# An attention and long-convolution kernel on Trainium2: the inverse transform's leftover matmuls as a step of their own, and a new order of all steps

## The chip, the cores and the metric

The kernel runs on one core of one Trainium2 chip. A core has a matrix engine (TensorE, in profiles PE, with its weight loads shown as PEld), three engines for elementwise work (VectorE or DVE, ScalarE or ACT, GpSimd or POOL), and SyncE (SP), which here only issues transfers. The matrix engine writes to PSUM, a memory of eight banks; DVE and ACT read results out of it. Each engine executes its own instructions in order and waits on semaphores for the others. The metric is the time of one execution in device microseconds, median of several runs.

## The reference, cut to what matters

Batch 8, 8 heads, 576 positions, head size 64. The first half is attention with a feature map of exponentials, the second a gated convolution by Fourier transforms along the 576 positions.

```
def phi(x):
    proj = np.einsum('bhsd,df->bhsf', x, w_phi)
    proj = proj - np.max(np.abs(proj), axis=-1, keepdims=True)
    return np.concatenate([np.exp(proj), np.exp(-proj)], axis=-1)
q_p, k_p = (phi(q), phi(k))
kv = np.einsum('bhsf,bhsd->bhfd', k_p, v)
z = np.sum(k_p, axis=2)
num = np.einsum('bhsf,bhfd->bhsd', q_p, kv)
den = np.einsum('bhsf,bhf->bhs', q_p, z)[..., None] + 1e-06
x = (num / den) as (8, 576, 512)
...
proj = x @ w_proj
x1, x2, x3 = (proj[..., :D].copy(), proj[..., D:2 * D].copy(), proj[..., 2 * D:].copy())
X2 = np.fft.rfft(x2, n=S, axis=1)
H = np.fft.rfft(filter_fft, n=S, axis=0)[None, :, :]
x2_conv = np.fft.irfft(X2 * H, n=S, axis=1)
y = x1 * x2_conv * x3
return (y @ w_out).astype(np.float32)
```

## The kernel before, in words

All of the work is a list of 1,538 words, the table `PLAN`. A word such as `I,3,1@2` names a method of the class `Kernel`, its arguments (first the batch, 0 to 7, then a chunk) and, after `@`, the PSUM bank that it uses. The method `run` walks through the list once and calls them, and each call issues its instructions to one engine. Nothing else orders the work: an engine executes its words as they stand in the list, and the framework adds the semaphores that the data and the banks need. So the list is the schedule of five engines at once, batches are interleaved in it, and the words also say which engine does a copy out of PSUM (`KVe,ACT,0,1`, `KVe,DVE,0,1`).

The methods that matter here, by batch:

- Attention. `load` and `loadh` bring q, k and v from memory (issued by POOL); `trh` transposes them by DMA (SP), in batch 0 `pt` does it on PE. `Pk`, `Qn`, `Pkt` and `Qnt` project k and q for the maxima `maxk` and `maxq` (DVE), `Pq` and `Pqt` project q again in the other layout, `ex`, `exkt` and `exqt` are the exponentials (ACT), `vs` scales v (POOL), `KV` forms the key-value sums, `KVe` copies them out, `NE` and `NEt` apply them to q, `rc` and `xn` divide (DVE).
- Forward. `f1` and `f2` add and subtract rows (POOL, some on DVE), `Fs` and `Ft` transform into the same two PSUM banks, `Fe` copies the spectrum XF out, `Xl` gathers its last columns. `X2` projects the spectrum, `Y1` multiplies by the filter, `m3` adds two products into T0 and T2; T4 is the product of the last 128 frequencies, 64 for each parity.
- Inverse and output. `I` transforms T0, T2 and T4 back for 128 channels: for each parity e one bank, two matmuls on T0 or T2 and one on T4. `Ie` copies one bank out (ACT), `Ip` and `Im` add and subtract (DVE), `X1`, `X3` with their tails `X1t`, `X3t` are the two gates, `tm` and `ym` multiply, `O` applies w_out, `Oe` copies out and `st` stores (SP).
- `wz` are matmuls on zeros that fill PE's time at the start; `Ff`, `H` and `He` prepare the filter in the first 50 us.

Two kinds of matmuls alternate on PE. `Pk`, `Qn`, `Pq`, `KV` and `Ft` contract over 64 rows and come in pairs, one on rows 0 to 63 and one on rows 64 to 127; the others contract over 128 rows. In `I` the T4 part multiplies all 128 rows of T4 for each parity by a table whose other 64 rows are zero: `inv` 4 and 5 get their sines with a scale column that is zero on the other half (lines 473 to 475). The class also has `It` and `Is`, the same work as two methods with T4's part first over 64 rows; no word of the list before calls them.

## Time and profile before

| | |
|---|---|
| median of 3 runs | 293.64 us |
| lowest, highest | 292.83 us, 295.11 us |
| span of the profiled execution | 291.2 us |
| instructions in the span | 10275 |
| granted clock of TensorE, mean | 0.996 |

The runs are timed from outside, so they stand above the span, which reaches from the first to the last instruction of one execution. The page's second part cuts that span into 40 slices of 7.3 us; each digit is the busy share of a slice in tenths.

```profile
PE   6688999998999999999999999999999899999992
DVE  6997898999889998998888987888999988787771
ACT  4999999987958778996897978967668988641421
POOL 8388794999968899999997999867949759955130
```

PE is full from the sixth slice nearly to the end, but in the first five it is not, and there ACT shows nines. The digits of DVE fall only at the very end. A busy share says nothing of who waits for whom; for that one reads, stage by stage, which engine has no idle time left. The chain that ended last, by engine and line:

```profile
PE 71%; DVE 3%; ACT 2%; issue 1%; DVEq 0%; ACTq 0%
PE ps L917 17%; PE ps L895 11%; PE ps L1016 10%; PE ps L970 8%; PE ps L773 5%; PE ps L787 4%; PE ps L876 3%; PE ps L926 2%; PE ps L670 2%; PE ps L636 2%; PE ps L643 2%; PE ps L676 2%; PE ps L869 2%; DVE mq L716 1%; PE ps L796 1%
```

L970 is the matmul of `I`, 8% of the chain; L869 is `Ft`, L917 the projections `X1` and `X3`, L895 `X2`, L1016 `O`.

### The profile page before, as it was taken

To read this page: it belongs to the slowest core of one execution; us is meant where nothing else is said; L and a number is where in the kernel's file an instruction comes from. 1 tells how busy PE (TensorE), PEld (TensorE's weight loads), DVE (VectorE), ACT (ScalarE), POOL (GpSimd) and SP (SyncE) were. 2 spreads that over 40 slices of the span, in tenths; PEclk is the share of its full clock that TensorE was granted. 3 is DMA by queue.
4 is the path that set the end of the run, shared out by engine and by line. 5 is a ranking of instruction groups with operands and counts; after the bars stand their busy time and mean duration, and the time that the engine had idled before them with its cause. 6 is when DMAs were issued, how large, how long until landed. Compare 5 with 4: busy or idle time off the path is not lost.

```text
span 291.2 us, 10275 instructions
## 1 busy us (share of the span) xinstructions
PE 274.0 (94%) x4336; PEld 194.8 (67%) x4336; DVE 252.3 (87%) x438; ACT 221.9 (76%) x367; POOL 228.5 (78%) x187
## 2 busy tenths in 40 slices
PE   6688999998999999999999999999999899999992
...
DVE  6997898999889998998888987888999988787771
ACT  4999999987958778996897978967668988641421
POOL 8388794999968899999997999867949759955130
...
GB/s 140 230 207 175 144 204 165 139 175 181 143 192 177 163 204 159 153 119 165 122 111 156 197 169 114 163 135 191 99 14 93 84 36 2 34 108 54 69 130 184
DMA packets 72319, 40.07 MB, mean 138 GB/s; under 512 B 52496, under 2 KB 67216, under 8 KB 72272
## 3 DMA queue, kind: packets, MB, share of 16 engines
...
q10 hardware_dynamic: 320, 0.52, 0.7%
...
## 4 chain that ended last, share of the span: by engine, by line
PE 71%; DVE 3%; ACT 2%; issue 1%; DVEq 0%; ACTq 0%
PE ps L917 17%; PE ps L895 11%; PE ps L1016 10%; PE ps L970 8%; PE ps L773 5%; PE ps L787 4%; PE ps L876 3%; PE ps L926 2%; PE ps L670 2%; PE ps L636 2%; PE ps L643 2%; PE ps L676 2%; PE ps L869 2%; DVE mq L716 1%; PE ps L796 1%
## 5 line engine op out<-in xcount | busy, mean ns | idle before, releaser
L917 PE MATMUL ps<-xT,wproj 128*128 128x256 bf16 x512 | 64.0, 273 | 0.2 <-DMA wproj<-in_moe_w_proj_dram 0.2
L917 PEld LDWEIGHTS <-wproj 128*128 128x128 bf16 x512 | 48.1, 98 | 9.0 <-DMA wproj<-in_moe_w_proj_dram 0.4
L1005 POOL TENSOR_TENSOR yT<-cv,x1s 128x576 bf16<-128x576 f32 x31 | 39.4, 1279 | 15.6 <-ACT es L988 7.7
L716 DVE TENSOR_REDUCE mq<-ps 128x8 f32<-128x1024 f32 (+1 forms) x40 | 43.7, 1112 | 3.5 <-PE ps L643 1.5
L716 DVE TENSOR_REDUCE mk<-ps 128x8 f32<-128x1024 f32 (+1 forms) x40 | 44.1, 1112 | 2.9 <-PE ps L636 1.6
L758 POOL TENSOR_TENSOR vm<-vn,vm 128x1152 bf16<-128x1152 bf16 x16 | 34.3, 2152 | 7.4 <-ACT vm L752 7.4
L758 POOL TENSOR_TENSOR vp<-vn,vp 128x1152 bf16<-128x1152 bf16 x16 | 34.4, 2155 | 4.6 <-ACT vp L752 4.5
L698 ACT ACTIVATE Eqp<-ps 128x1024 bf16<-128x1024 f32 x32 | 32.9, 1038 | 6.1 <-PE ps L676 6.0
L854 POOL TENSOR_TENSOR SD<-xn 128x512 bf16<-128x512 bf16 x28 | 31.9, 1153 | 6.2 <-DVE xn L806 4.7
L1016 PE MATMUL ps<-wout,yT 128*128 128x512 bf16 x140 | 34.8, 379 | 0.1
L860 POOL TENSOR_TENSOR xf<-SD 128x512 bf16<-128x512 bf16 x26 | 29.7, 1155 | 6.4 <-DVE SD L854 5.9
L698 ACT ACTIVATE Ekp<-ps 128x1024 bf16<-128x1024 f32 x32 | 33.2, 1036 | 1.1 <-PE ps L636 0.7
L698 ACT ACTIVATE Eqm<-ps 128x1024 bf16<-128x1024 f32 x32 | 32.6, 1037 | 1.6 <-PE ps L676 0.8
L698 ACT ACTIVATE Ekm<-ps 128x1024 bf16<-128x1024 f32 x32 | 33.1, 1033 | 0.8 <-PE ps L636 0.7
L895 PE MATMUL ps<-wproj,XF 128*128 128x512 bf16 x128 | 31.6, 379 | 0.3 <-ACT x1s L298 0.3
L991 DVE TENSOR_TENSOR cv<-es,ps 128x288 f32<-128x288 f32 x64 | 26.3, 445 | 5.7 <-ACT es L988 4.4
L909 POOL TENSOR_TENSOR T<-T,T 128x1024 bf16<-128x1024 bf16 x14 | 29.6, 2127 | 1.7 <-DVE r L801 0.8
L970 PE MATMUL ps<-inv,T 128*128 128x288 bf16 x192 | 28.1, 286 | 0.7 <-DVE mq L716 0.4
L958 DVE TENSOR_TENSOR x1s<-ps,x1s 128x512 bf16<-128x512 f32 x32 | 21.8, 685 | 2.5 <-PE ps L917 1.1
L298 ACT COPY o<-ps 128x512 f32<-128x512 f32 x20 | 11.8, 600 | 14.4 <-PE ps L1016 12.0
L806 DVE TENSOR_TENSOR xn<-ps,r 128x512 bf16<-128x512 f32 x32 | 21.9, 689 | 0.9
L298 ACT CAST x1s<-ps 128x512 bf16<-128x512 f32 (+1 forms) x33 | 17.4, 540 | 6.7 <-PE ps L917 3.2
(184 smaller groups left out, 635.5 us busy)
## 6 DMA issues: line engine op xcount, KB each, us to landing
...
wproj<-in_moe_w_proj_dram POOLq DMA_DIRECT2D x3, 512.0 KB, 8.7
...
```

Source lines behind the costliest of these rows:

```text
L298: self.nc.scalar.copy(dst, src)
L698: self.nc.scalar.activation(e, p, AF.Exp, bias=0.0, scale=1.0 if g == "p" else -1.0)
L716: self.nc.vector.tensor_reduce(out=out, in_=src, axis=AX.X, op=ALU.max, apply_absolute_value=True)
L758: self.eng(eng).tensor_tensor(out=t[:, :, :, 0:64], in0=self.at("vn", b)[:, 2 * X:2 * X + 2], in1=t[:, :, :, 64:65].to_broadcast([128, 2, ...
L854: self.eng(eng).tensor_tensor(out=o[:, :, 2 * i:2 * i + 2, :], in0=x[:, :, 0:2, :], in1=x[:, :, 2:4, :], op=ALU.subtract if i else ALU.add)
L860: self.eng(eng).tensor_tensor(out=o[:, :, 2 * i:2 * i + 2, :], in0=x[:, :, 0:4:2, :], in1=x[:, :, 1:4:2, :], op=ALU.subtract if i else ALU ...
L895: self.mm(self.pb(0), l, w[:, kt, 512:1024], start=(kt == 0), stop=(kt == 3))
L909: self.eng(eng).tensor_tensor(out=Y, in0=Y, in1=self.at(f"T{2 * e + 1}", b), op=ALU.add)
L917: self.mm(o[:, d], w[:, kt, f0 + 128 * m:f0 + 128 * m + 128], y[:, 1, ::-1, ::-1] if d else y[:, 0], start=(kt == 0), stop=(kt == 3))
L970: self.mm(self.pb(e, 0, 288), l, inv[:, 2 * e + i if i < 2 else 4 + e, :], start=(i == 0), stop=(i == 2))
L1005: self.eng(eng).tensor_tensor(out=self.at("yT", b)[:, m, 0:SEQ], in0=self.turn_of("cv", (b, m)).rearrange("p x h t -> p (x h t)"), in1=sel ...
L1016: self.mm(self.pb(0), y[:, kt, 128 * c:128 * c + 128], w[:, kt, :], start=(kt == 0), stop=(kt == 3))
```

## The change

The method `I` goes. Each of its 32 words becomes two: `Is`, the four matmuls on T0 and T2, and one for T4, either `It` (24 times), which takes for each parity only that parity's 64 rows, or `Iz` (8 times), which takes all 128 rows as `I` did. Either of the two may open the PSUM sum; a set `opened` remembers which came first, and that one starts the sum. `Ft` and `Fs` get the same freedom.

```
+    def opens(self, *key):
+        new = key not in self.opened
+        self.opened.add(key)
+        return new
...
     def Fs(self, b, v):
         xf, D = self.at("xf", b), self.at("D")
+        new = self.opens("F", b, v)
         for e in range(2):
             for s in range(2):
                 self.mm(self.pb(e, 144 * s, 144 * s + 144), xf[:, v, 2 * s + e, :],
-                        D[:, 288 * e + 144 * s:288 * e + 144 * s + 144], start=False,
-                        stop=(s == 1))
+                        D[:, 288 * e + 144 * s:288 * e + 144 * s + 144], start=new and s == 0,
+                        stop=not new and s == 1)
...
-    def I(self, b, m):
-        c, inv = slice(128 * m, 128 * m + 128), self.at("inv")
-        for e in range(2):
-            Y = self.at(f"T{2 * e}", b)
-            for i in range(3):
-                l = Y[:, i, c] if i < 2 else self.at("T4", b)[:, c]
-                self.mm(self.pb(e, 0, 288), l, inv[:, 2 * e + i if i < 2 else 4 + e, :],
-                        start=(i == 0), stop=(i == 2))
-
     def It(self, b, m):
-        c, inv = slice(128 * m, 128 * m + 128), self.at("inv")
+        c, inv, new = slice(128 * m, 128 * m + 128), self.at("inv"), self.opens("I", b, m)
         for e in range(2):
             r = slice(64 * e, 64 * e + 64)
-            self.mm(self.pb(e, 0, 288), self.at("T4", b)[r, c], inv[r, 4 + e, :], start=True,
-                    stop=False)
+            self.mm(self.pb(e, 0, 288), self.at("T4", b)[r, c], inv[r, 4 + e, :], start=new,
+                    stop=not new)
+
+    def Iz(self, b, m):
+        c, inv, new = slice(128 * m, 128 * m + 128), self.at("inv"), self.opens("I", b, m)
+        for e in range(2):
+            self.mm(self.pb(e, 0, 288), self.at("T4", b)[:, c], inv[:, 4 + e, :], start=new,
+                    stop=not new)
 
     def Is(self, b, m):
-        c, inv = slice(128 * m, 128 * m + 128), self.at("inv")
+        c, inv, new = slice(128 * m, 128 * m + 128), self.at("inv"), self.opens("I", b, m)
         for e in range(2):
             for i in range(2):
                 self.mm(self.pb(e, 0, 288), self.at(f"T{2 * e}", b)[:, i, c],
-                        inv[:, 2 * e + i, :], start=False, stop=(i == 1))
+                        inv[:, 2 * e + i, :], start=new and i == 0, stop=not new and i == 1)
```

The list itself is new from its first word to its last, 1,570 words instead of 1,538. Apart from I the same steps are there, with the same arguments, but in another order, on other banks, and with some of the copies on the other engine: KVe on DVE 8 times instead of 4, Fe 10 instead of 7, Xl 3 instead of 1, yt 3 instead of 1, Ffe 1 instead of 0, and Oe 12 instead of 15. Its last line but one before, and after:

```
-Oh,7,4,0@5 Oh,7,4,1@7 st,SP,7,2,1 st,ACT,7,0,0 Oeh,DVE,7,4,0@5 sth,SP,7,4,0 Oeh,DVE,7,4,1@7
+st,ACT,7,2,0 Oe,ACT,7,0@5 Oeh,DVE,7,4,0@3 sth,SP,7,4,0 st,ACT,7,0,0 Oeh,DVE,7,4,1@4 st,SP,7,0,1
```

Three places show how instructions move. The rows give the line of the kernel's file, the operation and what is written from what; a number behind a name tells buffers apart. The first place is PE in batch 4, the end of an inverse step: before, the second half of `I` (parity 1: T2, T2, T4) with the forward step `Ft` of batch 5 behind it.

```order
L970 LDWEIGHTS T20_1165
L970 MATMUL ps_61<-inv0_69,T20_1165 128x288
L970 LDWEIGHTS T40_1167
L970 MATMUL ps_61<-inv0_69,T40_1167 128x288
L869 LDWEIGHTS xnt1_132
L869 MATMUL ps_61<-Dt0_68,xnt1_132 128x288
```

And after, at the end of the `Is` of another chunk of batch 4: its `It` follows as a step of 64 rows, and a projection of k for batch 6, also of 64 rows, stands behind it.

```order
L985 LDWEIGHTS T20_1067
L985 MATMUL ps_61<-inv0_69,T20_1067 128x288
L972 LDWEIGHTS T40_1069
L972 MATMUL ps_61<-inv0_69,T40_1069 128x288
L633 LDWEIGHTS kT0_84
L633 MATMUL ps_61<-wphi0_62,kT0_84 128x128
```

T4's matmuls have left the middle of the step and stand at its end, next to other matmuls of 64 rows. The second place is DVE in the first 60 us, where batch 0's spectrum is multiplied by the filter (T from ps and HTo or HTe) and batch 2's maxima of k are taken (mk). Before:

```order
L905 TENSOR_TENSOR T20_1165<-ps_61,HTo0_71 128x1024
L716 TENSOR_REDUCE mk0_86<-ps_61 128x2x4
L905 TENSOR_TENSOR T30_1166<-ps_61,HTo0_71 128x1024
L716 TENSOR_REDUCE mk0_86<-ps_61 128x2x4
L905 TENSOR_TENSOR T00_1163<-ps_61,HTe0_70 128x1024
L962 TENSOR_TENSOR x1s0_141<-ps_61,x1s0_141 128x4x64
L905 TENSOR_TENSOR T10_1164<-ps_61,HTe0_70 128x1024
```

After:

```order
L713 TENSOR_REDUCE mk0_86<-ps_61 128x2x4
L909 TENSOR_TENSOR T20_1067<-ps_61,HTo0_71 128x1024
L297 CAST KVs1_123<-ps_61 128x2x260
L713 TENSOR_REDUCE mk0_86<-ps_61 128x2x4
L909 TENSOR_TENSOR T00_1065<-ps_61,HTe0_70 128x1024
L909 TENSOR_TENSOR T30_1068<-ps_61,HTo0_71 128x1024
L904 TENSOR_TENSOR T40_1069<-ps_61,H50_72 128x512
```

The copy of batch 1's key-value sums, KVs1, has come from ACT into the middle of DVE's row. The third place is DVE's end, batch 7's last half sums (cv), gates (x1s), the product yT and the copies of the output o. Before:

```order
L991 TENSOR_TENSOR cv1_1171<-es1_1169,ps_61 128x9x32 x2
L300 CAST x1s0_141<-ps_61 128x2x8x32
L958 TENSOR_TENSOR x1s0_141<-ps_61,x1s0_141 128x2x8x32
L1005 TENSOR_TENSOR yT1_1173<-cv1_1171,x1s0_141 128x576
L300 COPY o1_1175<-ps_61 128x512
L300 COPY yT0_1172<-yT1_1173 128x4x64
L300 COPY o4_1178<-ps_61 128x512
L300 COPY o5_1179<-ps_61 128x256 x2
```

After:

```order
L992 TENSOR_TENSOR cv1_1073<-es1_1071,ps_61 128x9x32 x2
L962 TENSOR_TENSOR x1s0_141<-ps_61,x1s0_141 128x2x8x32
L1006 TENSOR_TENSOR yT1_1075<-cv1_1073,x1s0_141 128x576
L297 COPY o0_1076<-ps_61 128x512
L297 COPY yT0_1074<-yT1_1075 128x4x64
L297 COPY o2_1078<-ps_61 128x512
L297 COPY o3_1079<-ps_61 128x512
L297 COPY o5_1081<-ps_61 128x256 x2
```

One gate's copy has left this place for ACT, and one more copy of the output has come.

More of the change, by code (lines that the diff above doesn't have):

```diff
@@ new lines @@
+cz,DVE,1 ident sin,9 cols_a wz,32@4 wz,33@3 wz,27@0 cols_b wz,9@2 fl_load,0,1 gi_nr ang,DVE,1 wz,31@6
+fl_load,2,0 loadh,k,0,0 loadh,k,0,1 fl_load,0,0 fl_load,3,0 w_phi wz,17@3 ang,ACT,3 fl_load,1,0
+pt,q,0,0,0@4 wz,35@7 one loadh,q,0,1 pt,q,0,0,1@5 frac,3 fl_load,3,1 cols_h wz,11@3 wz,5@1 wz,0@0
+pte,ACT,q,0,0,0@4 ang,DVE,2 frac,1 pte,DVE,q,0,0,1@5 Qn,0,1@6 frac,2 ang,DVE,0 load,v,0 load,q,1
+pt,k,0,0,0@0 zeros back frac,0 sin,3 sin,2 pte,DVE,k,0,0,0@0 pt,k,0,0,1@2 sin,1 fl_loadt wz,24@3 sin,0
@@ new lines @@
+Pk,0,0@4 pte,DVE,k,0,0,1@2 wz,30@3 exz maxq,0,1@6 Qn,0,0@2 Pk,0,1@6 ex,k,p,0,0@4 maxk,0,0@4 trh,q,1,0
+pt,k,0,1,0@1 maxq,0,0@2 pt,k,0,1,1@0 load,k,1 ex,k,m,0,0@4 ex,k,m,0,1@6 pte,ACT,k,0,1,0@1
+pte,ACT,k,0,1,1@0 trh,k,1,0 maxk,0,1@6 trh,q,1,1 trh,k,1,1 pt,q,0,1,1@5 pte,ACT,q,0,1,1@5 pt,q,0,1,0@4
+Pkt,0@0 pte,DVE,q,0,1,0@4 w_load,proj,0 w_load,out ex,k,p,0,1@6 maxkt,0@0 wz,34@2 exkt,p,0@0 Qn,0,3@2
+wz,14@4 fa,POOL,1 em,m,0,0 fa,POOL,0 load,k,2 maxq,0,3@2 Pk,0,3@6 em,p,0,0 Qnt,0@4 maxqt,0@4 exkt,m,0@0
@@ new lines @@
+f1,POOL,0,0,0 NE,0,3@0 maxq,1,0@6 rc,0,3@0 trx,0,1 ex,k,p,1,1@4 Pk,1,0@2 Ff,3@6 maxk,1,0@2 f2,POOL,0,0,0
+ex,k,p,1,0@2 Ffe,ACT,3@6 NE,0,2@4 ex,k,m,1,0@2 Ff,1@6 Qnt,1@2 xn,0,3@0 Pqt,0@0 rc,0,2@4 Ffe,ACT,1@6
+xn,0,2@4 maxqt,1@2 Qn,1,3@4 ptx,0,2@7 maxq,1,3@4 w_load,proj,2 ptx,0,0@2 ptxe,DVE,0,0@2 exqt,m,0@0
+ptxe,ACT,0,2@7 ptx,0,3@3 ptxe,DVE,0,3@3 trh,k,2,1 trh,k,2,0 Ff,0@6 exqt,p,0@0 f1,POOL,0,1,1 Qn,1,1@4
+load,v,2 f2,POOL,0,0,1 f1,POOL,0,1,0 maxq,1,1@4 trh,q,2,1 w_load,proj,1 Ffe,ACT,0@6 Pk,1,2@0 Qn,1,2@2
@@ new lines @@
+ex,k,p,1,2@0 f2,POOL,0,1,1 ex,k,m,1,2@0 X1,0,3@7 H,3@4 X1e,ACT,0,3@7 maxk,1,2@0 X1,0,2@5 X1,0,1@6
+NEt,0@0 He,ACT,3,1@4 He,ACT,3,0@4 trh,q,2,0 maxq,1,2@2 mhi,1 Pkt,1@2 X1e,ACT,0,2@5 X1e,DVE,0,1@6 rct,0@0
+xnt,0,0@0 H,0@7 X1,0,0@4 xnt,0,1@0 f2,POOL,0,1,0 Fs,0,2@5 Ft,0,1,0@5 maxkt,1@2 exkt,p,1@2 He,DVE,0,0@7
+exkt,m,1@2 Hl,ACT He,DVE,0,1@7 H,1@3 mlo,POOL,1 Fs,0,3@0 Fe,DVE,0,3@0 load,q,3 X3,0,1@2 trm,1@7
+He,DVE,1,1@3 em,m,1,0 Fe,ACT,0,2@5 X1e,ACT,0,0@4 Fs,0,1@5 H,2@4 trme,DVE,1@7 Ft,0,0,5@0 vs,POOL,m,1,0
```

312 lines of the change are left out of this document (145 added, 167 removed).

## The prediction

> **What bounds the kernel now.** I read the page's part 1 first, to see which engine is full; then the busy times by stretch, to see which engine ends the waits in each stage; then TensorE's timeline at single steps, to price a step and a change between row modes; then the groups by form, to price the copies that change engine.
>
> ```profile
> PE 274.0 (94%) x4336; PEld 194.8 (67%) x4336; DVE 252.3 (87%) x438; ACT 221.9 (76%) x367; POOL 228.5 (78%) x187
> ```
>
> TensorE (PE) is busy 94% of a span of 291.2 us. The average hides that other engines are full in some stages:
>
> ```profile
> core 0: us, PE busy (x) PEld busy (x) DVE busy (x) ACT busy (x) POOL busy (x), PEclk, DMA share, GB/s
> 12.00:40.00 28.00, 23.73 (x466) 16.04 (x461) 24.96 (x34) 27.55 (x42) 23.40 (x18) 1.00 1.25 182
> 40.00:77.00 37.00, 34.71 (x607) 25.68 (x607) 34.99 (x55) 33.50 (x59) 32.49 (x26) 1.00 1.19 170
> 77.00:222.00 145.00, 144.98 (x2350) 105.17 (x2343) 130.23 (x199) 114.65 (x193) 125.67 (x93) 1.00 0.95 147
> 222.00:235.00 13.00, 12.07 (x247) 8.58 (x247) 12.71 (x24) 12.78 (x20) 11.28 (x12) 1.00 0.38 61
> 235.00:262.00 27.00, 27.00 (x463) 20.65 (x461) 21.65 (x38) 17.79 (x32) 19.93 (x13) 1.00 0.22 44
> 262.00:286.00 24.00, 23.66 (x184) 15.40 (x181) 17.85 (x32) 7.79 (x17) 8.08 (x7) 1.00 0.43 94
> ```
>
> Read each row as stretch, length, then busy time per engine. From 12 to 40 us ACT is the bound (27.55 of 28.00; PE's 23.73 includes fillers). From 40 to 77 us PE (34.71 of 37.00) and DVE (34.99) share it. From 77 to 222 us PE idles 0.02 us in 145. From 222 to 235 us ACT and DVE bind; after that PE again. The granted clock is 1.00 throughout. So an order can win only where PE idles: 2.29 us (40 to 77), 0.93 (222 to 235) and 0.34 (the tail), plus what ACT sheds before 40. All else has to come out of PE's own work.
>
> **PE's work: price of a step and of a switch of rows.** In this timeline a step's cost is the distance to the next start, since matmuls overlap:
>
> ```profile
> 46.15 0.42 PE L869 MATMUL ps<-Dt,xnt 64*128 64x288 bf16 x4
> 46.41 0.39 PE L636 MATMUL ps<-wphi,kT 64*128 64x128 bf16 x8
> ...
> 190.73 0.90 PE L970 MATMUL ps<-inv,T 128*128 128x288 bf16 x6
> 191.47 1.04 PE L917 MATMUL ps<-xT,wproj 128*128 128x256 bf16 x8
> 192.34 0.63 PE L926 MATMUL ps<-xTt,wproj 128*128 128x64 bf16 x16
> 192.81 0.90 PE L970 MATMUL ps<-inv,T 128*128 128x288 bf16 x6
> 193.64 0.42 PE L869 MATMUL ps<-Dt,xnt 64*128 64x288 bf16 x4
> 193.99 0.64 PE L926 MATMUL ps<-xTt,wproj 128*128 128x64 bf16 x16
> ...
> 194.97 1.04 PE L917 MATMUL ps<-xT,wproj 128*128 128x256 bf16 x8
> 195.94 0.40 PE L636 MATMUL ps<-wphi,kT 64*128 64x128 bf16 x8
> ```
>
> An I step, six matmuls of 128 rows, takes 191.47 - 190.73 = 0.74 us, 0.123 each. The Ft step is the nearest row to the new It: the same 288 columns, 64 rows, halves on rows 0 to 63 and 64 to 127 in different banks. Followed by another 64-row step its four matmuls take 46.41 - 46.15 = 0.26, so two run side by side and a pair costs 0.13. A step of 128 rows takes 192.34 - 191.47 = 0.87 before another one of 128 rows, and 195.94 - 194.97 = 0.97 before one of 64. So a change of rows costs 0.10 us; the way back costs the same (Ft, 193.99 - 193.64 = 0.35 against 0.26).
>
> The change turns 32 I steps (192 matmuls) into 32 Is (128 matmuls, 15.7 us), 8 Iz (16 matmuls, 2.0) and 24 It (24 pairs, 3.1): 20.8 against 23.6, so **-2.8 us**. But walking through both lists and counting neighbours of different row modes gives 146 changes before and 170 after: 24 x 0.10 = **+2.4**. Some are Its between two steps of 128 rows; more come from the new order, which mixes the two kinds more finely. PE's work falls by **0.4 us**. The bounds: if the It pairs do not run side by side, 24 x 0.123 = 2.9 more; if a switch next to so short a step hides, 2.4 less. Which part of a sum comes first (Is or It, Fs or Ft) leaves PE the same matmuls; it only sets what the step waits for first, T4's product or the sums m3.
>
> The Trainium skill's TensorEngine Tiling (Array Packing), Key Properties, says that changing the tiling mode, not only the tile, drains TensorE; its TensorE: Matmul & The Clock Gate, Step-by-step, puts a drain at about 128 cycles, an estimate of 0.05 us at that page's 2.4 GHz. By that the switches would cost 1.3 us, and this term would be -1.5 instead of -0.4. The trace has the drain, at twice the price, and I go by the trace.
>
> **Copies that change engine.**
>
> ```profile
> L298 ACT CAST KVs<-ps 128x520 bf16<-128x520 f32 x12 | 7.3, 605 | 2.2 <-PE ps L773 2.1
> L300 DVE CAST KVs<-ps 128x520 bf16<-128x520 f32 x4 | 2.8, 698 | 1.4 <-PE ps L773 0.7 <-PE ps L683 0.7
> L298 ACT CAST XF<-ps 128x576 bf16<-128x576 f32 x25 | 15.2, 644 | 7.6 <-PE ps L876 7.6
> L300 DVE CAST XF<-ps 128x576 bf16<-128x576 f32 x7 | 5.2, 753 | 2.6 <-PE ps L876 2.6
> L300 DVE COPY o<-ps 128x512 f32<-128x512 f32 x15 | 10.3, 685 | 3.3 <-PE ps L1016 3.2
> L527 ACT ACTIVATE HF<-ps 128x576 bf16<-128x576 f32 x4 | 2.7, 687 | 0.0
> L300 DVE COPY XL<-XF 128x512 bf16<-128x512 bf16 x1 | 0.3, 283 | 0.0
> L300 DVE COPY yT<-yT 128x256 bf16<-128x256 bf16 x1 | 0.2, 216 | 0.0
> ```
>
> DVE gets 4 more KVe (2.8 us), 3 more Fe (2.3), 1 Ffe (taken as an XF cast of equal shape, 0.75), 2 Xl (0.57) and 2 yt (0.43), and gives up 3 Oe (2.06): **+4.8 us of DVE work**; ACT loses about as much. In the long stretch DVE is busy 130.23 of 145 us and covers its part. In the two full stages it matters where they land.
>
> *12 to 40 us.* ACT sheds an HF copy (0.687) and KVe 0,1 (0.605): up to -1.3. Against it, the second load, k's first half, is issued behind five more GpSimd instructions:
>
> ```profile
> 3.22 0.76 POOL L602 DMA_DIRECT2D kn<-in_k_dram  x1
> 3.99 0.41 POOL L332 IOTA fr<- 128x288 f32 x1
> 5.11 0.72 POOL L602 DMA_DIRECT2D qn<-in_q_dram  x1
> 10.24 0.68 PE L618 MATMUL ps<-ident,kn 128*128 128x128 bf16 x9 [1.49 <-DMA kn<-in_k_dram]
> 12.74 1.01 ACT L698 ACTIVATE Ekm<-ps 128x1024 bf16<-128x1024 f32 x1
> ```
>
> fr and idx2 take from 3.99 to 5.11, so that issue moves back 1.1 us, and PE already waited 1.49 us for this load. Between no delay (ACT works on the sine tables until the first exponential at 12.74) and 1.1, I take half: the term is -1.3 to -0.2, and I use **-0.6**.
>
> *The loads' queue.* On GpSimd's queue w_out and k, q, v of batch 2 are issued earlier, and the last two parts of w_proj fall behind them:
>
> ```profile
> wproj<-in_moe_w_proj_dram POOLq DMA_DIRECT2D x3, 512.0 KB, 8.7
> 34.69 0.76 POOL L586 DMA_DIRECT2D wproj<-in_moe_w_proj_dram  x1
> 49.49 1.03 PE L895 MATMUL ps<-wproj,XF 128*128 128x512 bf16 x4
> ```
>
> Issued at 34.69 and landed 8.7 us later, the last part now lies ready 6.1 us before X2 reads it. Three more loads stand ahead of it (15th instead of 12th); at the 170 GB/s of that stretch 576 KB take 3.5 us, so X2 starts 0 to 10.4 - 6.1 = 4.3 us late. I take **0**, since the loads ahead are issued earlier too. Stores and transposes on SP's queue keep their number, and no row of the long stretch shows PE waiting for one.
>
> *40 to 77 us.* KVe 1,0 and one x1s cast come to DVE, three copies of the filter's tables leave it; with 2.0 us of DVE idle as cover I take **0**. If every wait of PE went, -2.3; if the cover is gone, the order's next PE steps (KV's readers NE, and the Y1 products that free the banks) come late by what DVE gains.
>
> *222 to 235 us.* ACT sheds work, DVE gains some: **0**, between -0.9 and +0.9.
>
> *Tail.* The new list leaves two O steps of batch 6 as filler ahead of O,7,3, and that waits for DVE's last product:
>
> ```profile
> L958 DVE TENSOR_TENSOR x1s<-ps,x1s 128x512 bf16<-128x512 f32 x32 | 21.8, 685 | 2.5 <-PE ps L917 1.1 <-PE ps L744 1.0 <-ACT x1s L298 0.2
> L991 DVE TENSOR_TENSOR cv<-es,ps 128x288 f32<-128x288 f32 x64 | 26.3, 445 | 5.7 <-ACT es L988 4.4 <-POOL yT L1005 1.1
> 279.98 4.92 PE L1016 MATMUL ps<-wout,yT 128*128 128x512 bf16 x20
> 281.10 0.76 DVE L1005 TENSOR_TENSOR yT<-cv,x1s 128x576 bf16<-128x576 f32 x1
> ```
>
> From O,6,2 on DVE has one o copy, 4 x1s products, 8 half sums and the yT product: 0.685 + 2.74 + 3.56 + 0.76 = 7.75 us. PE has, up to O,7,3, four projections (3.5), two O (4.92/20 x 8 = 2.0), Iz and three Is (1.7), three It (0.4) and two switches (0.2): 7.8. They meet, so a wait of 0 to 0.6, where the tail idles 0.34 now: **+0.2**.
>
> Sum: -0.4 - 0.6 + 0 + 0 + 0.2 = -0.8 us. Against the profiled span that is 290.4. The median of the runs, 293.64, stands 2.4 us above the span, which I keep: **292.8 us**.
>
> **The rivals.**
>
> A, the forecast: the 2.8 us won by the pairs are paid back in switches, and the full stages stay full. 292.8, 290.7 to 296.6 (within 1%). Chance 0.50.
>
> B, the order pays: PE's idle time in 40 to 77 (2.29) and 222 to 235 (0.93) goes as well: 292.8 - 3.2 = 289.6. For it: 3.2 us of waits are there to be taken. Against: DVE has only 2.0 and 0.3 us of slack in these stages and gets more work. Chance 0.26.
>
> C, DVE becomes the bound, the slower side: all of the 4.8 us delays PE, 292.8 + 4.8 = 297.6. It decides once more than about 2 us lands between 40 and 77, or more than 0.3 between 222 and 235. Against: 145 us of slack at 90% lie between. Chance 0.13.
>
> D, copies stuck behind GpSimd. Before, the XL copy on DVE ran while GpSimd was idle:
>
> ```profile
> 49.13 0.28 DVE L300 COPY XL<-XF 128x512 bf16<-128x512 bf16 x1
> 50.25 2.15 POOL L758 TENSOR_TENSOR vm<-vn,vm 128x1152 bf16<-128x1152 bf16 x1 [4.34 <-ACT vm L752]
> ```
>
> No row shows such a copy beside a running GpSimd product. If it cannot start there, each of the four new ones waits up to 2.15 us with all of DVE's later work behind it: up to +8.6, half of that 297.1. The Trainium skill's SBUF, two separate sides, states such a lock: a DVE operation that uses the second port and a GpSimd operation exclude each other for a whole instruction. Chance 0.06.
>
> E, the change doesn't do what it says: It's two halves run one after the other, +2.9, 295.7. Against: Ft's rows. Chance 0.05.
>
> **How the numbers follow.** One per cent, about what a measurement of this kernel can tell from no change, is 2.9 us: below 290.7 or above 296.6. Faster is B, 0.26; same is A and E, 0.55; slower is C and D, 0.19. The range reaches to B's gain with the remaining 0.7 of the ACT term (288.9) and to C (297.6); outside lie the far part of D and a gain beyond every wait I can see.
>
> **What would show it.** In the profile after: It rows of 64 rows and 288 columns starting in pairs within 0.02 us, steps 0.13 apart (E wrong). Steps around them 0.10 longer at each change of rows. PE idle from 40 to 77 near 2.3 (B: near 0; C: above 4, with DVE over 36.5 busy). First exponential at about 12.7 us as now, else the k load counted. XL on DVE with a gap before it and GpSimd busy (D). I am wrong if PE shows waits in the middle stretch, where it has none now.

## The result, and the profile after

The changed kernel takes 339.82 us (median of 4 runs, 335.19 to 343.26) beside 293.77 for the kernel before on the same chip: ratio 1.1434, interval 1.1372 to 1.1495. The ratio leaves out runs in a disturbed state of the chip, so it lies below the quotient of the medians. The profiled execution took 335.19 us, with a span of 333.4 where 291.2 stood before: 42.2 us more.

The page's parts 1 and 2 of the changed kernel:

```profile
span 333.4 us, 10230 instructions
PE 285.7 (86%) x4303; PEld 200.8 (60%) x4336; DVE 261.5 (78%) x448; ACT 221.5 (66%) x357; POOL 229.9 (69%) x187
...
PE   8578687778886989899889986999999987999992
PEclk9769659999997999999999998999999999999999
```

PE's idle time rose from 17.2 us (291.2 - 274.0) to 47.7, so 30.5 of the 42.2 us are waits. The other 11.7 are, by estimate, the same work at a lower clock: busy time multiplied by the mean granted clock is 274.0 x 0.996 = 272.9 before and 285.7 x 0.953 = 272.3 after. PE's work is nearly the same; it is done later and, in the first quarter, slower. No other engine is full either: DVE fell from 87% to 78%. A kernel in which no engine is full is bound by the order in which the engines hand work to each other.

The busy times by stretch, in the columns of the prediction's table:

```profile
12.00:40.00 28.00, 20.66 (x346) 13.43 (x346) 20.62 (x26) 20.36 (x30) 19.97 (x14) 0.74 1.25 180
40.00:77.00 37.00, 29.81 (x399) 21.55 (x402) 27.71 (x38) 26.51 (x46) 19.99 (x16) 0.87 1.27 160
77.00:222.00 145.00, 127.54 (x2131) 92.25 (x2147) 116.49 (x178) 102.58 (x167) 113.23 (x85) 0.98 0.81 127
222.00:334.00 112.00, 99.58 (x1391) 69.98 (x1399) 88.95 (x151) 64.01 (x106) 66.91 (x48) 0.99 0.39 76
```

PE idles 7.34 us from 12 to 40 (4.27 before), 7.19 from 40 to 77 (2.29) and 17.46 from 77 to 222, where it idled 0.02. The granted clock, 1.00 in all these stretches before, is 0.74 in the first and 0.87 in the second.

The chain that ended last, by engine and by line, and some of its pieces in order of time (start, length, what):

```profile
PE 43%; DVE 18%; DMA 15%; ACT 14%; issue 5%; POOL 2%; SPq 1%; DVEq 0%; ACTq 0%; POOLq 0%
DMA kT<-kn 10%; PE ps L921 9%; DVE mk L713 7%; PE ps L899 7%; PE ps L1017 5%; DMA kn<-in_k_dram 5%; ACT Ekm L695 4%; PE ps L770 4%; ACT Ekp L695 4%; DVE mq L713 3%; PE ps L784 2%; PE ps L985 2%; PE ps L880 2%; PE ps L930 2%; PE ps L640 1%
```

```profile
8.73 15.39 DMA kn<-in_k_dram
24.14 12.53 DMA kT<-kn
...
45.83 20.27 DMA kT<-kn
...
181.13 1.03 ACT Ekp L695
182.19 1.24 DVE mk L713
183.45 1.02 ACT Ekm L695
```

Before, the chain was PE for 71% and no transfer stood among its first entries. Now it is PE for 43%, and two new kinds of rows stand in it. One is transfers: the load of a k and two transposes of k, 48 us in all. The other is a row of three at 181 us: an exponential (Ekp, ACT), the maximum (mk, DVE) and the other exponential (Ekm, ACT), each starting 0.02 to 0.03 us after the one ahead of it ended. All three read the same PSUM bank, the projection of k. In the groups of instructions, the column behind the second bar is the idle time ahead of them and what ended it. After:

```profile
L713 DVE TENSOR_REDUCE mk<-ps 128x8 f32<-128x1024 f32 x32 | 39.0, 1222 | 22.3 <-ACT Ekp L695 12.0 <-ACT Ekm L695 7.2 <-PE ps L633 3.0
L695 ACT ACTIVATE Ekp<-ps 128x1024 bf16<-128x1024 f32 x32 | 32.8, 1030 | 13.0 <-DVE mk L713 11.4 <-PE ps L633 1.4 <-ACT Eqp L695 0.3
L695 ACT ACTIVATE Ekm<-ps 128x1024 bf16<-128x1024 f32 x32 | 32.7, 1026 | 17.3 <-DVE mk L713 11.2 <-PE ps L633 4.6 <-PE ps L770 1.5
```

Before:

```profile
L716 DVE TENSOR_REDUCE mk<-ps 128x8 f32<-128x1024 f32 x32 | 39.0, 1219 | 2.9 <-PE ps L636 1.6 <-ACT Ekm L698 1.2
L698 ACT ACTIVATE Ekp<-ps 128x1024 bf16<-128x1024 f32 x32 | 33.2, 1036 | 1.1 <-PE ps L636 0.7 <-DVE mk L716 0.2
L698 ACT ACTIVATE Ekm<-ps 128x1024 bf16<-128x1024 f32 x32 | 33.1, 1033 | 0.8 <-PE ps L636 0.7
```

The instructions take as long as before. But DVE idled 22.3 us ahead of the maxima instead of 2.9, nearly all of it until an exponential ended, and ACT 30.3 us ahead of the exponentials instead of 1.9, most of it until a maximum ended. In both traces the two engines' reads of one of the 40 projections of k (four and a tail in each batch) never overlap. The Trainium skill's PSUM — Partial Sum Buffer, Terms, says that two engines on the same 32 partitions of one bank at once are an error, reads against reads included, so a program has to hold them apart; both traces agree, with 0 overlaps in 80 projections. Which of the three waits for which is then settled by the list. It has three forms: the maximum first (22 projections before, 11 after), last (13 and 13), or between the exponentials, ACT-DVE-ACT (5 before, 16 after). The last form has two hand-overs between the engines, the other two have one.

So there were two suspects, transfers at the start and readers of one bank, and with them the copies on DVE and the split of `I` itself. The experiments take them apart.

### The profile page after: what moved, and what is told of

Read it like the earlier page. It is cut to its first block, busy times and chain, and to the rows that moved or that the text cites. A ratio compares the mean times of both kernels' runs of the same rounds, so it can differ in the third digit from the quotient of the medians.

```text
span 333.4 us, 10230 instructions
## 1 busy us (share of the span) xinstructions
PE 285.7 (86%) x4303; PEld 200.8 (60%) x4336; DVE 261.5 (78%) x448; ACT 221.5 (66%) x357; POOL 229.9 (69%) x187
## 4 chain that ended last, share of the span: by engine, by line
PE 43%; DVE 18%; DMA 15%; ACT 14%; issue 5%; POOL 2%; SPq 1%; DVEq 0%; ACTq 0%; POOLq 0%
DMA kT<-kn 10%; PE ps L921 9%; DVE mk L713 7%; PE ps L899 7%; PE ps L1017 5%; DMA kn<-in_k_dram 5%; ACT Ekm L695 4%; PE ps L770 4%; ACT Ekp L695 4%; DVE mq L713 3%; PE ps L784 2%; PE ps L985 2%; PE ps L880 2%; PE ps L930 2%; PE ps L640 1%
## 5 line engine op out<-in xcount | busy, mean ns | idle before, releaser
L921 PE MATMUL ps<-xT,wproj 128*128 128x256 bf16 x512 | 65.9, 278 | 2.6 <-ACT XF L295 1.6
L921 PEld LDWEIGHTS <-wproj 128*128 128x128 bf16 x512 | 49.3, 99 | 12.4 <-issue 3.4
L1017 PE MATMUL ps<-wout,yT 128*128 128x512 bf16 x127 | 33.4, 379 | 2.7 <-DVE mT L297 1.0
L899 PE MATMUL ps<-wproj,XF 128*128 128x512 bf16 x115 | 29.8, 380 | 1.0 <-issue 0.3
L992 DVE TENSOR_TENSOR cv<-es,ps 128x288 f32<-128x288 f32 x64 | 25.6, 443 | 1.4 <-ACT es L989 0.8
L295 ACT CAST x1s<-ps 128x512 bf16<-128x512 f32 (+1 forms) x32 | 17.2, 546 | 13.6 <-PE ps L921 8.6
L784 PE MATMUL ps<-KVs,Eqp 128*128 128x65 bf16 x256 | 20.9, 196 | 1.7 <-DVE mk L713 0.7
L1017 PEld LDWEIGHTS <-yT 128*128 128x128 bf16 x140 | 12.7, 98 | 15.1 <-issue 2.9
## 6 DMA issues: line engine op xcount, KB each, us to landing
wproj<-in_moe_w_proj_dram POOLq DMA_DIRECT2D x3, 512.0 KB, 14.3
```

The lines of the kernel that those rows point to most:

```text
L784: self.mm(self.pb(u, 65 * a, 65 * a + 65), E, KVs[:, u, v, s, :], start=(s == 0), stop=(s == 1))
L899: self.mm(self.pb(0), l, w[:, kt, 512:1024], start=(kt == 0), stop=(kt == 3))
L921: self.mm(o[:, d], w[:, kt, f0 + 128 * m:f0 + 128 * m + 128], y[:, 1, ::-1, ::-1] if d else y[:, 0], start=(kt == 0), stop=(kt == 3))
L992: self.nc.vector.tensor_tensor(out=self.turn_of("cv", (b, m))[:, :, odd, :], in0=self.turn_of("es", (b, m)).rearrange("p (x t) -> p x t", ...
L1017: self.mm(self.pb(0), y[:, kt, 128 * c:128 * c + 128], w[:, kt, :], start=(kt == 0), stop=(kt == 3))
```

## The experiments

Ratios are to the kernel before, timed on the same chip, with 95% intervals. Theory R is the readers of a bank, theory L the loads and transposes of the start; others are named as they come.

**Directions and loads in the changed list (flip, loads, both).** `flip` turns 15 of the 16 ACT-DVE-ACT projections of the changed list into one of the other forms; nothing else moves:

```diff
-ex,k,p,0,0@4 maxk,0,0@4 trh,q,1,0 ... ex,k,m,0,0@4
+maxk,0,0@4 ex,k,p,0,0@4 trh,q,1,0 ... ex,k,m,0,0@4
```

> The changed kernel, with 15 of its 40 k projections read in another order: each projection in PSUM is read by DVE (maximum, 1.22 us) and twice by ACT (exponentials, 1.03 us each), and in neither trace do these reads overlap, each waits for the one ahead of it in the list. After has 16 projections with DVE's read between ACT's two, before 5; here 1. Every engine keeps its own row of instructions. Theory R (readers): ACT's waits for DVE's maxima (27 us in all) and DVE's for ACT's exponentials (20 us) hold up the copies out of PSUM and so PE in the long stretch; the kernel gains 6 to 20 us of the 46. Rival N (no lead): the waits are only where a schedule without lead shows, and move elsewhere; gain under 2 us. Rival S (start): the loss comes from late transfers before 77 us; gain under 2 us.

Measured: 344.65 us, 1.1550 (1.1474 to 1.1626): no gain; the ratio stands 1.2 points above the changed kernel's, with intervals that touch. `loads` puts the loads and transposes of batch 1's k ahead of q's, w_proj's first part and w_out later, and k of batch 3 ahead of batch 4's:

```diff
-load,v,0 load,q,1 ... load,k,1 ... w_load,proj,0 w_load,out
+load,v,0 load,k,1 ... load,q,1 ... w_load,proj,0 load,q,2 ... load,q,3 w_load,out
-trh,q,1,0 ... trh,k,1,0 trh,q,1,1 trh,k,1,1
+trh,k,1,0 ... trh,k,1,1 trh,q,1,0 trh,q,1,1
```

> The changed kernel, with its first loads and transposes nearly in the order of before: k of batch 1 ahead of q, w_proj's first part and w_out no longer between them, k of batch 3 ahead of k of batch 4, the two transposes of k of batch 1 first. Theory S (start): after's PE is 17 us behind before's at the key-value sums of batch 1 (69.7 against 52.3 us), mostly because k's transposes of batches 1 and 2 land 12.5 and 20.3 us after their issue; with this order the sums of batch 1 start 7 to 14 us earlier and the whole is as much shorter. Theory R: that place is late because of the order in which k is read too, and gains 0 to 5 us. Rival N: the later waits take it back, gain under 2 us.

Measured: 334.72 us, 1.1347 (1.1291 to 1.1402). The first `KV,1,0` comes at 61.8 us instead of 69.7, but the next one, `KV,1,1`, at 77.4 as without the edit (77.3). In between PE waits 6.8 us, once, for another transpose, xTt. Both edits together:

> The two edits of the runs before this one in one kernel. If R and S act at different places, the gains add up, 13 to 34 us less than the changed kernel. If one wait hides behind the other, it is no better than the better of the two. If N holds, under 4 us.

Measured: 345.87 us, 1.1708 (1.1617 to 1.1799). In a list whose engines are late already, neither repair does what its theory expected. A load brought forward delays another one. And the waits between the readers do not go away with the form: `both` has one ACT-DVE-ACT projection where `loads` has 16, yet in its trace ACT idles 24.6 us ahead of the two exponentials until a maximum ended (17.9 in `loads`), and DVE 16.5 us ahead of the maxima until an exponential ended (19.8). So the number of such projections is no price by itself; how close the list puts the readers likely counts too, which no run here tried alone. Whether the suspects are guilty is asked next in the kernel before, where nothing else is late.

**Readers in the kernel before (ada, ada_late).** `ada` turns 9 more projections of the list before into ACT-DVE-ACT:

```diff
-maxk,0,0@4 maxq,0,1@0 fl_load,3,1 fl_load,2,0 ex,k,p,0,0@4
+ex,k,p,0,0@4 maxk,0,0@4 maxq,0,1@0 fl_load,3,1 fl_load,2,0
```

> The kernel before, with 9 more of its k projections read by ACT, then DVE, then ACT (14 instead of 5), each engine's own row of instructions unchanged. Theory R: slower, by up to 9 times 1.2 us if nothing else covers the stop, so 2 to 11 us. Rival N: within 1 us of before, since the readers' order is no cause by itself.

Measured: 312.40 us, 1.0551 (1.0447 to 1.0655). `ada_late` moves only the six of them that lie behind the start, by moving one word for each. One of them:

```diff
-Pk,2,1@6 ex,k,p,2,1@6 ex,k,m,2,1@6 ... maxk,2,1@6 load,v,2
+Pk,2,1@6 ex,k,p,2,1@6 ... maxk,2,1@6 ex,k,m,2,1@6 load,v,2
```

> The kernel before, with only the six later of ada's nine projections (two of batch 2, two of batch 4, one of 5, one of 7; after 54 us) read by ACT, then DVE, then ACT; six words of the list moved, every engine's own row unchanged. Theory R: each such reading stops ACT for up to the maximum's 1.2 us and DVE for the exponential's 1.0; 3 to 8 us slower, with PE idle in 77 to 222 us. Rival: ada's loss came from its first three projections and the late transfers, so within 1.5 us of before.

Measured: 303.14 us, 1.0304 (1.0230 to 1.0379). Six words out of 1,538, no instruction more or less, cost 3.0%, 9.4 us of medians. The stretch from 77 to 222 us and two groups of `ada_late`:

```profile
77.00:222.00 145.00, 139.21 (x2261) 100.72 (x2282) 124.58 (x187) 113.64 (x187) 124.15 (x92) 1.00 0.98 146
```

```profile
L698 ACT ACTIVATE Ekp<-ps 128x1024 bf16<-128x1024 f32 x32 | 33.2, 1038 | 6.2 <-DVE mk L716 5.2 <-PE ps L636 1.0
L698 ACT ACTIVATE Ekm<-ps 128x1024 bf16<-128x1024 f32 x32 | 33.1, 1035 | 7.6 <-DVE mk L716 6.8 <-PE ps L636 0.7
```

ACT's idle time ahead of the two exponentials rose from 1.9 to 13.8 us, 12.0 of it until a maximum ended, and PE idles 5.79 us in the stretch where it idled 0.02. R has a price in this list: 1.6 us for each of the six readings.

**No shared bank at all (nsa, nsb).** Here the maxima of k are left out: the same reduction reads zeros in SBUF, with the same duration (median 1.209 us), so no projection of k has readers on two engines. `nsa` is the changed kernel, `nsb` the one before:

```diff
-                    self.db().rearrange("p a (i f) -> p a i f", i=4))
+                    self.at("zz")[:, 0:1].to_broadcast([128, 2, 4, 128]))
```

> The changed kernel, with the 40 maxima of k taken from a tile of zeros in SBUF instead of the projection in PSUM: same instructions, same row on every engine, but DVE and ACT no longer read the same bank. It leaves out the maxima of k, so the output is another. Theory R (readers of one bank wait for each other): most of the loss of the long stretch goes, 18 to 30 us less than the changed kernel's 339.8, about 310 to 322. Rival N (an order without lead): the maxima come no later than before, all other waits stay, gain under 5 us. Rival C (the copies moved to DVE): DVE has the same work, gain under 5 us.

> The kernel before, with the same edit (maxima of k from SBUF; it leaves them out too). Theory R: its list already lets the readers of k wait little (DVE 4 us and ACT under 1 us in all, mostly hidden), so within 2 us of before. If this kernel gains as much as the changed one does by the edit, the edit helps for another reason than R.

Measured: `nsb` 293.92 us, 0.9994 (0.9962 to 1.0026): before, the shared bank costs nothing that shows, which fits the little idle time ahead of its readers. `nsa`: 331.24 us, 8.6 less than the changed kernel by medians where 18 to 30 were expected; its runs scatter from 321.69 to 333.87 and give no interval. The run that was traced took 332.01 us and shows waits that moved: PE waits 8.4 us for the transpose xTt in the start, where the changed kernel's longest single wait is 2.8. All four runs lie below the lowest of the changed kernel (335.19), so R holds in sign; its size is not settled by this run.

**The split alone (split, free).** The list before with `I` replaced by the pair that the changed list uses for that chunk, nothing else moved:

```diff
-xn,1,1@4 I,0,2@2 em,p,2,0
+xn,1,1@4 Iz,0,2@2 Is,0,2@2 em,p,2,0
```

> The order, banks and copies of before, with each I word replaced by the two words that the changed kernel has for that chunk (Is with It or Iz, in its sequence). The prediction's sum for PE: 24 pairs save 24 x 0.12 us = 2.9, and a change of rows more costs 0.10 us each: 24 It words between steps of 128 or 64 rows; between -2.9 and +2.0 us against before. If the split itself were the cause of the loss, it would be over 10 us slower.

Measured: 296.45 us, 1.0090 (1.0064 to 1.0116). In this list PE changes rows 182 times instead of 146, so by the prediction's prices its work grows by 0.8 us (36 x 0.10 - 2.8); by the ratio the kernel loses 2.7. `free` uses `It` only where a step of 64 rows stands beside it already (11 of 32), on that side, and `Iz` elsewhere, so that the split adds no change of rows:

> The order, banks and copies of before, with I split only where a step of 64 rows stands next to it: 11 of 32 become It with Is, with It beside that step, so that no change of rows is added (146, as before); the other 21 take all 128 rows. 11 pairs save 11 x 0.12 = 1.3 us of PE's work. If PE bounds the long stretch, 291 to 293.5 us, ratio 0.992 to 0.998; if the waits for DVE and ACT take it back, within 0.2% of before.

Measured: 295.76 us, 1.0061 (1.0023 to 1.0099). PE's busy time multiplied by the clock falls from 272.9 to 272.2 us, where 1.3 were priced, and the kernel is still slower: from 77 to 222 us PE now idles 2.3 us. A likely reason stands in the row of the copy `Ie` (tile es), before and in `free`:

```profile
L988 ACT COPY es<-ps 128x288 f32<-128x288 f32 x32 | 12.9, 404 | 12.0 <-PE ps L970 8.9 <-ACT es L988 1.0 <-ACT Ekp L698 0.7
```

```profile
L989 ACT COPY es<-ps 128x288 f32<-128x288 f32 x32 | 12.8, 400 | 15.4 <-PE ps L978 7.6 <-PE ps L972 2.6 <-issue 1.1
```

`I` finished parity 0's bank after three matmuls, and ACT copied it while PE did parity 1. In the pair both banks close only with the second step: the median time from a chunk's first matmul to the start of its copy goes from 0.62 us to 0.87, and ACT idles 3.4 us more ahead of the 32 copies. This small loss comes with the split itself; that the copy is its cause was not tested by a run of its own.

**The weights' place in the loads (bl).** The list before with only w_proj's first part and w_out loaded at about 9 us (before: 31.25 and 58.09) and batch 1's q ahead of its k, as the changed list does:

```diff
-load,v,0 ... load,k,1 ... load,q,1 fa,POOL,0 ... w_load,proj,0 ... w_load,out
+load,v,0 ... load,q,1 ... load,k,1 w_load,proj,0 w_load,out fa,POOL,0 ...
```

> The kernel before, with one thing of the changed list alone: the first part of w_proj and w_out are loaded right behind q and k of batch 1, with q ahead of k, instead of at 31 and 58 us. Theory S: 1 MB more stands ahead of k of batch 2 and competes with k of batch 1, whose transposes come 3 to 6 us later; 3 to 9 us slower. Rival N: hidden behind ACT's work in 12 to 40 us, within 1.5 us of before.

Measured: 306.59 us, 1.0415 (1.0296 to 1.0535). Two of its stretches, and PE's longest wait:

```profile
12.00:40.00 28.00, 20.86 (x402) 14.28 (x404) 20.71 (x28) 23.11 (x34) 18.65 (x13) 0.94 1.27 193
40.00:77.00 37.00, 30.31 (x506) 22.77 (x508) 28.49 (x41) 28.72 (x51) 23.92 (x18) 0.91 0.82 122
```

```profile
PE ps L636 <- DMA kT<-kn: 8.6, 2, 5.1
```

L has its price too. PE waits 8.6 us, in two waits, for transposes of k for which it never waited before. And the granted clock fell from 1.00 to 0.94 and 0.91 in stretches where only loads had moved: the low clock follows PE's waits, and adds to them.

**Start and rest (h_start_before, h_start_after).** Two lists spliced at the first inverse step of batch 0 (63.9 us before, 80.5 in the changed kernel): `h_start_before` is the list before up to there and the changed order from there on, `h_start_after` the other way round:

```diff
+(words of the list before, up to the first step of I) load,k,4 trh,k,3,0 em,p,2,0 exkt,m,2@0 load,v,3 Iz,0,2@2 Is,0,2@2
```

> The list of before up to the first inverse step of batch 0 (62.6 us in its trace; I taken as Is with It or Iz), then the remaining words of the changed list, with its banks and copies. Theory S (start) with R and D (long stretch): the changed kernel reaches this point about 17 us later than before and loses some 25 us behind it; here only the second loss is left, 312 to 324 us. If all loss comes from the start, 293 to 299; if none does, 335 or more.

> The other way round: the changed list up to the first inverse step of batch 0 (some 80 us in its trace), then the remaining words of before. Only the first loss is left: 308 to 318 us. If it adds up, the excess of this run and of the run before it over 294 make the 46 us of the change.

Measured: the changed start alone costs 7.5% (319.71 us, 1.0750, 1.0664 to 1.0836), the changed rest alone 11.7% (328.80 us, 1.1174, 1.1120 to 1.1227). Together 19.2%, more than the 14.3% of the whole change. The seam of `h_start_before` is a likely reason: 17 words lie there between the load of batch 3's k and its first transpose (36 in the changed list), and in its trace PE waits 8.2 us for a transpose of q and 5.1 us for two of x. The changed kernel's trace has no wait of PE for either, so the 11.7% are probably not the changed rest's own loss alone.

**The rest taken apart (h1n, h1nx, h1nxt).** `h1n` is `h_start_before` with the maxima of k left out as in `nsa`:

> The run h_start_before, with the maxima of k read from zeros in SBUF (they are left out of the result). Theory R: what the long stretch loses is mostly the wait of ACT and DVE for each other at the projections of k; 294 to 304 us. Rival D (copies held up behind GpSimd) or N: stays within 5 us of h_start_before.

Measured: 315.79 us, 1.0739 (1.0680 to 1.0799): the readers are 4.4 of the 11.7 points. What DVE did in a stretch of `h1n`, and POOL beside it (start, duration):

```profile
191.42 5.91 DVE L297 COPY yT<-yT 128x256 bf16<-128x256 bf16 x1
```

```profile
190.91 4.25 POOL L755 TENSOR_TENSOR vm<-vn,vm 128x1152 bf16<-128x1152 bf16 x2
195.11 2.14 POOL L755 TENSOR_TENSOR vp<-vn,vp 128x1152 bf16<-128x1152 bf16 x1
```

A copy that took 0.216 us before takes 5.91: it ends at 197.33, just after the third of GpSimd's products (195.11 + 2.14 = 197.25), and PE then waits 4.2 us for the DVE product behind it. This is the prediction's rival D, in a list whose readers of k no longer wait for each other. `h1nx` puts the copies `Xl` and `yt` of this list back on ACT:

```diff
-Xl,DVE,3 ... yt,DVE,3 ... Xl,DVE,4 ... yt,DVE,5
+Xl,ACT,3 ... yt,ACT,3 ... Xl,ACT,4 ... yt,ACT,5
```

> The run h1n, with the seven or fewer Xl and yt copies that DVE has put back on ACT. Theory D (rival D of the prediction: such a copy does not start while GpSimd runs a product; in the changed kernel's trace the XL and yT copies last up to 0.69 us instead of 0.22 to 0.28, and with the maxima off PSUM one yT copy lasted 5.9 us): 2 to 6 us less than h1n. Rival: ACT has 0.4 us more per copy and DVE less, within 1 us of h1n.

Measured: 309.31 us, 1.0523 (1.0478 to 1.0567): the copies are 2.2 points, 6.5 us, in this list. In `h_start_before`, with the maxima computed, the same seven copies last only 0.7 us longer in all than at the durations of before. What is left are transposes, in SP's queue and on PE:

```profile
SPq L605 <- DMA kn<-in_k_dram: 17.8, 1, 17.8
```

```profile
PE ps L640 <- DMA qT<-qn: 8.2, 1, 8.2
PE ps L921 <- DMA xT<-xn: 5.2, 2, 3.7
```

SP stands 17.8 us on a transpose whose load has not landed, and the transposes behind it wait with it. `h1nxt` gives SP's transposes and POOL's loads behind the splice about the order that they have before:

```diff
-trh,k,3,0 ... trh,k,3,1 trh,q,3,0 trx,1,1 ... trh,q,3,1 ... trx,1,0
+trx,1,1 ... trh,q,3,1 ... trx,1,0 trh,q,3,0 ... trx,1,2 trh,k,3,1 trh,k,3,0
```

> The run h1nx, with SP's transposes and the loads of k and q behind the seam in nearly the order of before: in h1nx SP waited 17.8 us for k of batch 3 with the transposes of q of batch 3 and of x of batch 1 queued behind it, and PE then waited 8.2 us for q and 5.2 us for x. Theory S: these waits go, 10 to 14 us less than h1nx (309.3), so 295 to 299. Rival N: the waits are taken by the next late operand, 305 or more.

Measured: 310.39 us, 1.0516 (1.0432 to 1.0600): nothing gained. The wait for q fell to 2.0 us and another stands in its place, 6.7 us in `KV` for POOL's product vp.

**Two more repairs (h1best, loads2).** `h1best` is `h_start_before` with `Xl` and `yt` on ACT and other read directions, all maxima computed. Its list reads nine of the 40 projections in another order, not the 18 that its expectation names, and 15 of 17 stay ACT-DVE-ACT. `loads2` is `loads` with xTt's transpose ahead of those of batch 2's q, and w_out and k of batch 4 later still:

```diff
-exkt,m,3@6 maxkt,3@6 exkt,p,3@6
+exkt,m,3@6 exkt,p,3@6 maxkt,3@6
```

> The run h_start_before (328.8, maxima of k from PSUM again, result complete), with Xl and yt on ACT as in h1nx and other directions for the reads of k: 18 of the 40 projections are read in another order by DVE and ACT, every engine keeps its own row. h1n to h1nx says 6.5 us for the copies. Theory R: another 4 to 8 us for the directions, so 314 to 319. If the directions do nothing, 322.

```diff
-maxq,1,1@4 trh,q,2,1 w_load,proj,1 ... trh,q,2,0 ... tm,0,1@2 trxt,0
+maxq,1,1@4 w_load,proj,1 ... tm,0,1@2 trxt,0 trh,q,2,1 trh,q,2,0
```

> The run loads, and in addition: the transpose of the last rows of batch 0 (xTt) is issued ahead of the two transposes of q of batch 2, w_out and k of batch 4 are loaded later. In loads PE waited 7.0 us at X1t for xTt, which stood 14.8 us in SP's queue behind these two and then took 14.4 us. Theory S (transfers at the start): 5 to 8 us less than loads (334.7), so 327 to 330. Rival N: the next wait takes its place, within 2 us of loads.

Measured: `h1best` 321.28 us, 1.0835 (1.0725 to 1.0946), 3.4 points below `h_start_before`. The rows of the exponentials in `h_start_before`, and in `h1best`:

```profile
L695 ACT ACTIVATE Ekm<-ps 128x1024 bf16<-128x1024 f32 x32 | 33.0, 1032 | 9.7 <-DVE mk L713 5.8 <-PE ps L633 3.6
L695 ACT ACTIVATE Ekp<-ps 128x1024 bf16<-128x1024 f32 x32 | 33.0, 1036 | 10.1 <-DVE mk L713 9.0 <-PE ps L633 0.8 <-ACT Eqp L695 0.3
```

```profile
L695 ACT ACTIVATE Ekm<-ps 128x1024 bf16<-128x1024 f32 x32 | 33.0, 1032 | 9.3 <-PE ps L633 6.0 <-DVE mk L713 3.3
L695 ACT ACTIVATE Ekp<-ps 128x1024 bf16<-128x1024 f32 x32 | 33.0, 1033 | 5.3 <-DVE mk L713 4.3 <-PE ps L633 1.0
```

ACT's idle time until a maximum ended falls from 14.8 us to 7.6, and the copies that moved were held 0.7 us in `h_start_before`. So most of the gain is likely the directions'; the two edits were not run apart. `loads2` 332.36 us, 1.1192 (1.1073 to 1.1311): 1.6 points below `loads`, 4.6 us, a little under the 5 to 8 expected. The run that was traced took 333.12 us; in it PE waits for w_proj (4.6 us, 2 waits) and for q's transpose (3.0). No version beats the kernel before.

## Why the prediction was wrong

**The premise.** "So an order can win only where PE idles" is true, but I took from it that an order can also lose little: 0 for 40 to 77 us, nothing at all for the long stretch. The 0.02 us of idle PE from 77 to 222 were a property of the old list, not of the work. With a list that is new from end to end that row is no longer evidence, and the whole stretch was open: 17.46 us of idle PE came there. Its own test, "I am wrong if PE shows waits in the middle stretch, where it has none now", came true.

**Readers of one bank.** The prediction has no term for them, since the row of mk before shows only 2.9 us of idle time. That row shows that the waits were covered by the order, not that there was nothing to wait for. The lists could be counted: ACT-DVE-ACT 5 times before, 16 times after. Shown: 3.0% for six more of them in the kernel before, and 4.4 points when DVE's readings are all taken out of the changed rest. Not shown: that turning the form back in the changed list helps (`flip` and `both` gained nothing), so the count is a warning and not a price.

**"The loads' queue ... I take 0", bounds 0 to 4.3.** I priced the one load that falls behind, w_proj's last part, and not those that are issued earlier. In the changed kernel POOL's queue has the weights right behind k of batch 1:

```profile
8.73 0.75 POOL L593 DMA_DIRECT2D kn<-in_k_dram  x1
9.46 0.79 POOL L583 DMA_DIRECT2D wproj<-in_moe_w_proj_dram  x1
10.24 0.75 POOL L586 DMA_DIRECT2D wout<-in_moe_w_out_dram  x1
```

Two loads of 512 KB go out within 1.6 us of the k that PE needs next; that k lands 15.39 us after its issue (the chain), and its first transpose starts at 24.1 us instead of 21.4. The transposes kT of the first 80 us, duration in nanoseconds (least, median, most) and time to landing, before:

```profile
L608 SPq DMA_TRANSPOSE kT<-kn x5: 1950/2135/2281, 21.4 to 77.3; - x5
DMA to landing us min/median/max: 5.9/6.4/8.1
```

After:

```profile
L605 SPq DMA_TRANSPOSE kT<-kn x6: 1296/4441/8302, 24.1 to 78.9; - x6
DMA to landing us min/median/max: 5.0/15.7/20.3
```

`KV,1,0`, at 52.3 us before, starts at 69.7. The bytes moved per second are much the same (180 and 160 GB/s in the two stretches, 182 and 170 before): what differs is which transfer stands first. Shown: 4.1% by these loads alone (`bl`), 7.5% by the whole changed start. How the remaining 3.4 points divide between readers and other moves there stays open; the three early projections that `ada` has and `ada_late` has not make 2.5 of `ada`'s 5.5.

**The first stage, "-0.6".** Its sign was wrong. ACT's first two rows of exponentials in the changed kernel:

```profile
13.78 1.02 ACT L695 ACTIVATE Ekp<-ps 128x1024 bf16<-128x1024 f32 x1 [0.97 <-PE ps L633]
16.10 1.94 ACT L695 ACTIVATE Ekm<-ps 128x1024 bf16<-128x1024 f32 x2 [1.29 <-DVE mk L713]
```

The first exponential starts at 13.78 us instead of 12.74, 1.04 later: the upper bound of the load's delay (1.1), of which I had taken about half (half of 1.1 would have made the term -0.75, not -0.6). Behind it ACT idles 1.29 us more until the maximum has read the bank, which no term had.

**Rival D (0.06).** The mechanism was there: in the kernel before, none of the 15 copies and sums that DVE makes between bf16 tiles in SBUF overlaps a running GpSimd product, and in the changed kernel they meet them. The size was not: in the changed kernel the six XL and yT copies of DVE last 0.8 us longer in all than at the durations of before, where D had 4.3. The 6.5 us of `h1nx` are near that by luck: they belong to another list, and most of them to the one copy of 5.91 us. What D did not name is DVE's sums xf, six before and six after: they take 5.4 us instead of 2.5. Whether a copy or sum meets a product can be read off the two engines' rows in the list. A row of DVE in the changed kernel, and what POOL did beside it:

```profile
98.21 1.36 DVE L857 TENSOR_TENSOR xf<-SD 128x512 bf16<-128x512 bf16 x1
```

```profile
98.43 0.75 POOL L593 DMA_DIRECT2D qn<-in_q_dram  x1
```

Alone such a sum took 0.415 us before. A reader who looks for idle time doesn't find these waits: they stand in the duration of the DVE instruction. The Trainium skill's SBUF — State Buffer, two separate sides, states the lock, and the copy in `h1n` agrees (5.91 us). For a DVE operation with two SBUF inputs, as this sum is, the page names only a GpSimd operation that reads SBUF; here the sum was held while GpSimd issued loads.

**PE's work, "-0.4".** Right in its prices. Three steps of the changed kernel:

```profile
256.69 0.30 PE L972 MATMUL ps<-inv,T 64*128 64x288 bf16 x2
256.93 0.66 PE L985 MATMUL ps<-inv,T 128*128 128x288 bf16 x4
257.43 1.04 PE L921 MATMUL ps<-xT,wproj 128*128 128x256 bf16 x8
```

The pair of `It` takes 256.93 - 256.69 = 0.24 us ahead of a step of 128 rows, 0.13 for the pair and 0.10 for the change, and `Is` 0.50 for four matmuls, 0.12 each. Between two steps of 64 rows the median of `It` is 0.123. So rival E falls, and busy time times clock (272.9 and 272.3, 0.6 less) is near the sum. What the term lacked is a cost of the split beside PE's work, likely the copy `Ie`, which now waits for the second step: the kernel before with the split alone is 0.6 to 0.9% slower.

**Rivals B and C, and the tail.** B needed waits to vanish. C, DVE as the bound, is not it: DVE's busy time rose by 9.2 us, of which 3.8 are the held copies and sums (and two `trme` and one `X1te` came to DVE, one `He` and one `ptxe` left it, which no term counts), but it is busy 78% of the span and 27.71 of 37.00 us from 40 to 77, where C asked for more than 36.5. In the tail PE waits for nothing that the trace names after 310 us; that term, +0.2, was harmless.

**The sum.** Start 7.5, readers of the rest 4.4 and copies 2.2 make 14.1 points, beside the 14.3 measured. That is no account and the nearness is chance: the parts were measured in other surroundings than the changed kernel's own, and the copies are held only 0.8 us there. What the rest still costs in `h1nx` (5.2 points, with PE waiting 8.2 us for q's and 5.2 for x's transposes) belongs in part to the seam, it seems, since the changed kernel shows no such wait. How the changed kernel's 42.2 us divide between readers, transfers and the steps' other moves stays open; the copies KVe, Fe and Oe on other engines and the other banks were not tried alone.
